# A cached attention step with a gated MLP: the per-head sums behind the next unit's first turns, and the MLP's first half at the head

## The chip, the cores and the metric

The kernel runs on one core of a Trainium2 chip. The metric is device time in microseconds for one execution; a profiled execution also gives a span, from the first to the last instruction. The engines are TensorE (PE, with its weight loads PEld), VectorE (DVE), ScalarE (ACT), GpSimd (POOL) and SyncE (SP), which here only issues transfers. They run on their own and meet through semaphores.

## The reference

```python
x  = A_x                                   # 2 rows of 512, bfloat16
xn = layernorm(x)
# attention over a cache: 2 batches, 32 query heads, 8 key heads, 32768 positions, head width 128
q = (xn @ wq)                              # 512 -> 4096
p = softmax(q . k_cache / sqrt(128))       # 4 query heads share a key head
s = (p @ v_cache) @ wo                     # 4096 -> 512
# MLP on one position: the shifted heads are all padding, so w1 and w2 add nothing
x1 = xn                                    # B: x + hs, hs = 0
h2 = gelu(layernorm(x1) @ w3) @ w4         # 512 -> 1792 -> 512, gelu by tanh
out = x + s * silu(x1 + h2)
```

With one position per sequence the shift by one or two positions leaves zeros, so `hs` is zero and the kernel reads neither w1 nor w2.

## The kernel before, in words

The caches are 16 units, one for each pair of batch and key head; unit n has batch n % 2 and key head n // 2. Each unit has 8192 KB of K and 8192 KB of V. A partition holds 256 positions; the layout in memory is position-major, so a transfer is a plain copy.

**Buffers.** `kbuf` has room for three halves of a K (each of CW = 16384 columns); even units use the first two thirds, odd units the last two, and the shared third is worked on first. `vbuf` holds one V, no more. The weights borrow these: wq lies in the last third of `kbuf` until the queries are made; w3 and w4 lie in the first third and wo in the second once the last units are through with them.

**Head.** `layernorm` (L364), transposition of xn and of its normalised copy (`xT`), the setting up of selection matrices and the clearing of PSUM tiles on VectorE (L400 to L418), then `q_job` (L420): 128 narrow matmuls in a loop, a selection by `pick`, a copy to `qp` (L447) and a clearing of hP (L449). `place_q(n)` (L451) puts the four query heads of unit n into `qz`, where zeros stand around them, by four copies on ScalarE, one for each block of 32 partitions.

**A unit** (loop at L547):

- `scores(n)` (L459): two halves of four turns. A turn (L465) is a transposition of 32x32 blocks on VectorE from `kbuf` to one of two buffers `ktb`; eight matmuls (L477) with `qz` follow on TensorE. So turn t + 2 waits for the scores of turn t.
- `load_k(n + 1)` is issued by SyncE once the four turns of the first half have read the shared third.
- `softmax(n)` (L486): `place_q(n + 1)`, maximum (L490), a transposition of the maxima, their spread over partitions, exp with sums on ScalarE (L500), the transposition pT (L506), 1/sum (rS, L507).
- `values(n)` (L509): 64 matmuls from `vbuf` into `acc`. `load_v(n + 1)` is issued when they end, as `vbuf` is then free.
- `unit_end(n)` (L527): VectorE multiplies `acc` by rS and a mask (acs, L530) and adds four parts (acr, L534); TensorE makes the heads' outputs (ot, L537) and ScalarE copies them into oQ (L539).

**Order.** Every engine works in the order in which the operations were recorded. `Plan.op` finds the waits from the regions read and written; `emit_looped` folds equal rounds of TensorE (each unit) and VectorE (each pair of units, the last pair written out) into loops, in which `fit` writes a wait's value as a line in the loop's counters. All loads of K, V and weights stand in one SyncE stream in this order: wq, K(0), V(0), K(1), V(1), ..., K(15) in two halves, V(15), w3, w4, four pieces of wo, the output.

**Tail.** After the last unit: `mlp_in` (L569, 16 matmuls with w3 into hP), the turn of oQ (oT, L581), perm (L585), gelu in six operations on ScalarE and VectorE (L590 to L597), its transposition `h_turn` (L600) and copy h_bf (L606), `mlp_out` (L610) with w4, the wo products (`wo_rows`, `wo_last`) between them, the gate, the product and the two output transfers.

Of the kernel before, what the change touches and what calls it, by code (L numbers as in the profile page):

```python
# [8 lines left out]
BF16 = mybir.dt.bfloat16  # L9
U32 = mybir.dt.uint32  # L10
ACT = mybir.ActivationFunctionType
ALU = mybir.AluOpType
# [14 lines left out]
class Plan:  # L27
# [69 lines left out]
    def fit(self, points, first):  # L97

        i1 = min(i for i, _ in points if i > first)
        line, early, ahead = {}, {}, {}  # L100
        for s in sorted({s for (i, _), w in points.items() if i > first for s in w}):
            js = sorted({j for (i, j), w in points.items() if i == i1 and s in w})
            step = self.step[s]
            if js != sorted({j for i, j in points if i == i1}):
                assert js == [0]
                early[s] = (points[i1, 0][s] - (i1 - first) * step, step)
                got = {k: early[s][0] + (k[0] - first) * step for k in points if k[1] == 0}
            else:
                v0 = points[i1, js[0]][s]
                jstep = points[i1, js[1]][s] - v0 if len(js) > 1 else 0  # L110
                line[s] = (v0 - (i1 - first) * step, step, jstep)
                got = {k: line[s][0] + (k[0] - first) * step + k[1] * jstep for k in points}
            for k, v in got.items():
                if k[0] > first:
                    assert points[k].get(s) == v, (s, k, v, points[k])
                assert v > 0
                if k[0] == first and points[k].get(s, 0) > v:
                    ahead[s] = max(ahead.get(s, 0), points[k][s])
        for k, w in points.items():
            for s, v in w.items():  # L120
                if k[0] == first and s not in line and s not in early:
                    ahead[s] = max(ahead.get(s, 0), v)
        return line, early, ahead

    def emit_looped(self, eng, kind):
# [22 lines left out]
        for seg in segments:  # L148
            fits = []
            for q, places in enumerate(seg):  # L150
                assert len({r[p].label for r in rounds for p in places}) == 1
                line, early, a = self.fit(
                    {(i, j): r[p].waits for i, r in enumerate(rounds) for j, p in enumerate(places)}, 0)
                assert not early or q == 0
                fits.append((line, early))
# [9 lines left out]
        with self.nc.Fori(0, len(rounds), 1, engines=[kind], hint_back_edge=True) as i:  # L165
            for seg, fits in zip(segments, plans):
                if len(seg[0]) == 1:
                    o, (line, _) = rounds[0][seg[0][0]], fits[0]
                    self.emit_one(o, [(s, i * step + base) for s, (base, step, _) in line.items()])
                    continue  # L170
                for s, (base, step) in fits[0][1].items():
                    e.wait_ge(self.sems[s], i * step + base)
                with self.nc.Fori(0, len(seg[0]), 1, engines=[kind]) as j:
                    for places, (line, _) in zip(seg, fits):
# [9 lines left out]
def kernel(  # L184
# [38 lines left out]
    W4 = DK * Fdim  # L223
    HW = NHALF * GT * 32 // 2
    assert NCH == 2 and NB == NS and NU % 2 == 0 and FK <= 16 and W4 + FK * D <= CW
# [8 lines left out]
    def sb(name, shape, dt, align=32):  # L234
        return nc.alloc_sbuf_tensor(name, shape, dt, align_bytes=align).ap()
# [15 lines left out]
    qz = sb("qz", [128, 4, QW], BF16)  # L251
    qp = sb("qp", [128, 4, B, Hkv, rep], BF16)
# [12 lines left out]
    oQ = sb("oQ", [128, B, NR], BF16)  # L265
    oT = sb("oT", [128, B, NR], BF16)
# [184 lines left out]
    def place_q(n):  # L451
        b, g = n % 2, min(n // 2, Hkv - 1)
        for i in range(4):
            c0 = 32 - rep + 32 * i
            act(lambda i=i, c0=c0: A.copy(  # L455
                out=qz[32 * i:32 * i + 32, :, c0:c0 + rep], in_=qp[32 * i:32 * i + 32, :, b, g, :]),
                ["qp"], [("qz", i, i + 1)])

    def scores(n):  # L459
        for h, c in enumerate(halves(n % 2)):  # L460
            P.inner = h
            for t in range(NB // KG):
                i = t % KTB
# [63 lines left out]
    def unit_end(n):  # L527
        b, g = n % 2, n // 2
        ot = mA[:, 136:136 + rep]
# [6 lines left out]
            ["acs"], ["acr"], "acr")  # L536
        pe(lambda: T.matmul(ot, lhsT=acr[:, :], rhs=headm[:, :], start=True, stop=True),  # L537
           ["acr", "headm"], ["mA"], "ot")
        act(lambda: A.copy(out=oQ[:, b, g * rep:(g + 1) * rep], in_=ot), ["mA"], [("oQ", n, n + 1)])  # L539

    q_job()
    place_q(0)

# [3 lines left out]
    for n in range(NU):  # L547
# [3 lines left out]
        if n + 1 < NU:  # L551
            load_k(n + 1)
        softmax(n)
# [3 lines left out]
        unit_end(n)  # L557
        for s in ("PE", "DVE", "ACT"):
# [9 lines left out]

    def mlp_in():  # L569
        w3 = w3_s.rearrange("p k (q f) -> p k f q", f=FK)  # L570
        for k in range(DK):
            for j in range(4):
                f0, f1 = 4 * j, min(4 * j + 4, FK)
                r = T.matmul(
                    hP[32 * j:32 * j + B, 0:(f1 - f0) * 128].rearrange("p (f q) -> p f q", q=128),
                    lhsT=xT[:, DK + k, :], rhs=w3[:, k, f0:f1, :],
                    start=(k == 0), stop=(k == DK - 1), tile_position=(0, 32 * j))
        return r

    pe(mlp_in, [kreg(0, W4), "xT"], ["hP"])  # L580
    dve(lambda: V.transpose(  # L581
        out=oT[:, :, :].rearrange("p b r -> p (b r)"), in_=oQ[:, :, :].rearrange("p b h -> p (b h)")),
        ["oQ"], ["oT"])
    oPp = mA[:, 0:B * NR]
    pe(lambda: T.matmul(  # L585
        oPp, lhsT=perm[:, :, :].rearrange("p h a -> p (h a)"),
        rhs=oT[:, :, :].rearrange("p b r -> p (b r)"), start=True, stop=True), ["perm", "oT"], ["mA"])
    dve(lambda: V.tensor_copy(out=oP[:, :, :].rearrange("p b r -> p (b r)"), in_=oPp), ["mA"], ["oP"])

    act(lambda: A.activation(out=x2[:, :], in_=hP[:, :], func=ACT.Square), ["hP"], ["x2"])  # L590
    dve(lambda: V.tensor_scalar(
        out=x2[:, :], in0=x2[:, :], scalar1=0.044715, scalar2=1.0, op0=ALU.mult, op1=ALU.add), ["x2"], ["x2"])
    dve(lambda: V.tensor_mul(out=x2[:, :], in0=hP[:, :], in1=x2[:, :]), ["hP", "x2"], ["x2"])
    act(lambda: A.activation(out=th[:, :], in_=x2[:, :], func=ACT.Tanh, scale=GELU_C), ["x2"], ["th"])
    dve(lambda: V.tensor_scalar(
        out=th[:, :], in0=th[:, :], scalar1=0.5, scalar2=0.5, op0=ALU.mult, op1=ALU.add), ["th"], ["th"])
    dve(lambda: V.tensor_mul(out=h_row[:, :], in0=hP[:, :], in1=th[:, :]), ["hP", "th"], ["h_row"])  # L597
    hT = hP.bitcast(BF16)[:, 0:512]

    def h_turn():  # L600
        for s in range(4):
            r = T.transpose(out=hT[:, s * 128:(s + 1) * 128], in_=h_row[:, s * 128:(s + 1) * 128], identity=ident[:, :])
        return r

    pe(h_turn, ["h_row", "ident"], ["hP"])
    dve(lambda: V.tensor_copy(  # L606
        out=h_bf[:, :, :].rearrange("p (j s) b -> p j s b", j=4),
        in_=hT.rearrange("p (s j c) -> p j s c", s=4, j=4)[:, :, :, 0:B]), ["hP"], ["h_bf"])
# [39 lines left out]
    pe(mlp_out, [kreg(W4, FK * D), "h_bf"], ["mD"])  # L648
# [60 lines left out]
```

## Time and profile before

| | us |
|---|---|
| median of three runs | 667.06 (665.47 to 668.28) |
| the profiled execution | 667.29 |
| its span | 665.5 |
| PE busy | 412.8 |
| DVE busy | 381.0 |
| ACT busy | 41.3 |
| POOL busy | 2.0 |
| HBM read | 280.50 MB, 421 GB/s over the span |

A row of the timeline reads: start, length, engine, line of the kernel, operation, output <- input with shapes, count of merged instructions, and in brackets the engine's idle time before it with what ended it. A row of the chain has start, length, and what was worked or waited on. For transfers the profile gives the issue (an instruction of SyncE of 0.3 to 0.6 us) and the time from issue to landing.

### The profile page before, as it was taken

To read this page: it belongs to the slowest core of one execution; us is meant where nothing else is said; L and a number is where in the kernel's file an instruction comes from. 1 tells how busy PE (TensorE), PEld (TensorE's weight loads), DVE (VectorE), ACT (ScalarE), POOL (GpSimd) and SP (SyncE) were. 2 spreads that over 40 slices of the span, in tenths; PEclk is the share of its full clock that TensorE was granted. 3 is DMA by queue.
4 is the path that set the end of the run, shared out by engine and by line. 5 is a ranking of instruction groups with operands and counts; after the bars stand their busy time and mean duration, and the time that the engine had idled before them with its cause. 6 is when DMAs were issued, how large, how long until landed. Compare 5 with 4: busy or idle time off the path is not lost.

```text
span 665.5 us, 6187 instructions
## 1 busy us (share of the span) xinstructions
PE 412.8 (62%) x2397; PEld 162.9 (24%) x2397; DVE 381.0 (57%) x304; ACT 41.3 (6%) x124; POOL 2.0 (0%) x11
## 2 busy tenths in 40 slices
PE   1766764856746485664658466464847646485864
PEld 1532221322212132221223222121312212132321
DVE  5057673827457382745748284673828467385833
ACT  1001010010101001010100101010010101001011
POOL 1000000000000000000000000000000000000000
PEclk9999897877779787786968778797977879797877
DMA  9999999999999999999999999999999999999992
GB/s 379 441 441 390 390 421 437 441 441 441 441 441 430 390 441 441 441 441 441 418 402 441 441 441 441 441 441 441 418 402 441 441 441 441 441 410 473 418 397 101
DMA packets 5815, 280.55 MB, mean 422 GB/s; under 512 B 682, under 2 KB 692, under 8 KB 948
## 3 DMA queue, kind: packets, MB, share of 16 engines
q1 hardware_dynamic: 5768, 280.50, 97.7%
q8 instruction: 2, 0.03, 0.0%
q10 hardware_dynamic: 44, 0.01, 0.0%
q14 instruction: 1, 0.01, 0.0%
HBM read 280.50 MB, written 0.00 MB: 421 GB/s over the span
## 4 chain that ended last, share of the span: by engine, by line
DMA 55%; PE 19%; DVE 18%; issue 6%; ACT 1%; another core or an unknown queue 1%; DVEq 0%; ACTq 0%; SPq 0%
DMA kbuf<-in_A_k_cache_dram 55%; DVE ktb L465 14%; PE sc L477 12%; PE mA L428 3%; PE acc L518 2%; DVE m L490 1%; ACT pr L500 1%; PE wP L631 0%; DVE pT L506 0%; DVE acs L530 0%; DVE acr L534 0%; PE mD L613 0%; DMA x_bf<-in_A_x_dram 0%; DVE stats L366 0%
## 5 line engine op out<-in xcount | busy, mean ns | idle before, releaser
L477 PE MATMUL sc<-ktb,qz 128*128 128x512 bf16 x1024 | 272.5, 416 | 124.6 <-DVE ktb L465 122.4
L465 DVE STREAM_TRANSPOSE ktb<-kbuf 128x2048 uint32<-128x2048 uint32 x128 | 286.5, 2287 | 84.9 <-DMA kbuf<-in_A_k_cache_dram 59.0
L477 PEld LDWEIGHTS sc<-ktb,qz 128*128 128x128 bf16 x1024 | 96.9, 103 | 293.8 <-issue 152.4
L518 PE MATMUL acc<-vbuf,pT 128*16 128x512 bf16 x1024 | 86.4, 512 | 13.7 <-DVE rS L507 13.7
L530 DVE SCALAR_TENSOR_TENSOR acs<-acc,rS,mask 128x512 f32<-128x512 f32 x16 | 12.0, 751 | 88.7 <-PE acc L518 88.7
L518 PEld LDWEIGHTS acc<-vbuf,pT 128*16 128x16 bf16 x1024 | 31.0, 113 | 62.5 <-issue 52.4
L455 ACT COPY qz<-qp 32x16 bf16<-32x16 bf16 x68 | 13.7, 201 | 426.9 <-PE sc L477 393.4
L490 DVE TENSOR_REDUCE m<-sc 128x1 f32<-128x1024 f32 x16 | 19.6, 1224 | 32.0 <-PE sc L477 32.0
L506 DVE STREAM_TRANSPOSE pT<-pr 128x1024 bf16<-128x1024 bf16 x16 | 19.9, 1245 | 20.4 <-ACT pr L500 20.4
L537 PE MATMUL mA<-headm,acr 128*128 128x4 f32 x32 | 6.3, 268 | 30.7 <-DVE acr L534 30.7
L428 PE MATMUL mA<-xT,kbuf 128*128 128x2 bf16 x128 | 17.7, 183 | 11.7 <-issue 6.7
L503 PE MATMUL mA<-S,headf 128*128 128x1 f32 x32 | 7.9, 318 | 23.8 <-ACT pr L500 23.8
L500 ACT ACTIVATE pr<-sc,nb 128x1024 bf16<-128x1024 f32 x16 | 17.8, 1114 | 29.5 <-DVE nb L499 29.5
L491 PE MATMUL mA<-identf,m 128*1 128x128 f32 x16 | 4.3, 270 | 21.1 <-DVE m L490 21.1
L428 PEld LDWEIGHTS mA<-xT,kbuf 128*128 x128 | 13.3, 104 | 16.1 <-issue 13.1
L534 DVE TENSOR_REDUCE acr<-acs 128x128 f32<-128x512 f32 x16 | 16.3, 1018 | 0.6
L537 PEld LDWEIGHTS mA<-headm,acr 128*128 128x128 f32 x32 | 4.9, 194 | 38.8 <-DVE acr L534 38.8
L435 DVE CAST q_sb<-mA 128x64 bf16<-128x64 f32 x1 | 0.2, 225 | 24.8 <-PE mA L428 24.8
L503 PEld LDWEIGHTS mA<-S,headf 128*128 128x128 f32 x32 | 6.6, 257 | 25.2 <-ACT pr L500 25.2
L496 PE MATMUL mA<-ones_f,gx 1*128 1x1 f32 x32 | 6.5, 268 | 9.9 <-DVE gx L494 9.9
L539 ACT CAST oQ<-mA 128x4 bf16<-128x4 f32 x16 | 2.6, 162 | 146.6 <-PE mA L537 146.6
L491 PEld LDWEIGHTS mA<-identf,m 128*1 128x1 f32 x16 | 1.3, 79 | 29.0 <-DVE m L490 29.0
(84 smaller groups left out, 63.3 us busy)
## 6 DMA issues: line engine op xcount, KB each, us to landing
kbuf<-in_A_k_cache_dram SPq DMA_DIRECT2D x2, 4096.0 KB, 22.6
kbuf<-in_A_wq_dram SPq DMA_DIRECT2D x1, 4096.0 KB, 12.2
kbuf<-in_B_w_dram SPq DMA_DIRECT2D x2, 1792.0 KB, 30.7
kbuf<-in_A_wo_dram SPq DMA_DIRECT2D x1, 2048.0 KB, 32.0
kbuf<-in_A_wo_dram SPq DMA_DIRECT2D x1, 1280.0 KB, 29.4
kbuf<-in_A_wo_dram SPq DMA_DIRECT2D x1, 512.0 KB, 30.2
vbuf<-in_A_v_cache_dram SPq DMA_DIRECT2D x16, 25.6
kbuf<-in_A_wo_dram SPq DMA_DIRECT2D x1, 256.0 KB, 30.4
```

The lines of the kernel that those rows point to most:

```text
L428: r = T.matmul(qT[:, bass.ds(h2 * (2 * B) + e * B, B)], lhsT=kb[:, bass.ds(h2 * (2 * Dh) + (2 * CW + k * HD + e * Dh), Dh)], rhs=xT[:, k, ...
L455: act(lambda i=i, c0=c0: A.copy(out=qz[32 * i:32 * i + 32, :, c0:c0 + rep], in_=qp[32 * i:32 * i + 32, :, b, g, :]), ["qp"], [("qz", i, i ...
L465: dve(lambda i=i, c0=c0: V.transpose(out=ktb[i][:, :], in_=kbuf[:, c0:c0 + KG * GT * Dh].bitcast(U32)), [kreg(c0, KG * GT * Dh)], [f"ktb{i ...
L477: r = T.matmul(sc[:, bass.ds(half, HW)].rearrange("p (t k) -> p t k", k=32), lhsT=qz[:, k, off:off + 128], rhs=kv[:, k // 2, k % 2, :, :], ...
L490: dve(lambda: V.tensor_reduce(out=m1[:, :], in_=sc[:, :], axis=AX.X, op=ALU.max), ["sc"], ["m1"], "max")
L500: act(lambda: A.activation(out=pr[:, :], in_=sc[:, :], func=ACT.Exp, bias=nb[:, 0:1], scale=inv_sqrt_dh, accum_out=S1[:, :]), ["sc", "nb"] ...
L503: pe(lambda: T.matmul(sS, lhsT=headf[:, :, :].rearrange("p x h -> p (x h)"), rhs=S1[:, :], start=True, stop=True), ["headf", "S1"], [rO], "S")
L506: dve(lambda: V.transpose(out=pT[:, :, :].rearrange("p t r -> p (t r)"), in_=pr[:, :]), ["pr"], ["pT"], "pT")
L518: r = T.matmul(acc[32 * j:32 * j + 16, :].rearrange("p (i d) -> p i d", d=Dh), lhsT=pT[:, half * GT + u, r0:r0 + 16], rhs=vv[:, x, u, :, : ...
L530: dve(lambda: V.scalar_tensor_tensor(out=acs[:, :, :], in0=acc[:, :].rearrange("p (i d) -> p i d", d=Dh), scalar=rS[:, 0:1], in1=mask[:, : ...
L534: dve(lambda: V.tensor_reduce(out=acr[:, :], in_=acs[:, :, :].rearrange("p i d -> p d i"), axis=AX.X, op=ALU.add), ["acs"], ["acr"], "acr")
L537: pe(lambda: T.matmul(ot, lhsT=acr[:, :], rhs=headm[:, :], start=True, stop=True), ["acr", "headm"], ["mA"], "ot")
```

## The change

- `unit_end` is split. `unit_sum(n)` (acs and acr) is recorded within `scores(n + 1)`, behind the second turn of its first half; `unit_out(n)` (ot and its copy) behind those scores and ahead of `softmax(n + 1)`. Unit 0 so works on an empty unit before it, whose product goes to a spare tile; rS is cleared for it. The last unit's sums come after the loop.
- w3 is loaded behind wq into the first half of `vbuf`. V(0) comes in two halves: the second half (c = 1) behind K(0), the first one behind `mlp_in`, which now follows the first `place_q`.
- gelu's six operations are recorded right after the loop, so they follow exp(15) on ScalarE and rS(15) on VectorE. `h_turn` and h_bf stand ahead of the last `unit_sum`.
- w4 goes to the start of `kbuf` and is loaded directly behind V(15).
- `place_q` is one multiplication on GpSimd, of `qp` spread over four blocks by the new mask qm, made by a reduction on VectorE at the head.
- `fit` no longer has a separate list of waits ahead of an inner loop: a wait found for the first pass alone is written with step zero.

```diff
+    def load_v0_half(c):
+        load("v", vbuf[:, c * CW:(c + 1) * CW], cache(A_v_cache, 0)[:, c * CW:(c + 1) * CW],
+             [("vbuf", c * CW, (c + 1) * CW)])
...
-    w3_s = kbuf[:, 0:W4].rearrange("p (k f) -> p k f", k=DK)
-    w4_s = kbuf[:, W4:W4 + FK * D].rearrange("p (f d) -> p f d", f=FK)
+    w3_s = vbuf[:, 0:W3].rearrange("p (k f) -> p k f", k=DK)
+    w4_s = kbuf[:, 0:FK * D].rearrange("p (f d) -> p f d", f=FK)
 
     load("wq", wq_s, wq_v, [kreg(2 * CW, CW)])
+    load("w3", w3_s, w3_v, [("vbuf", 0, W3)])
     load_k(0)
-    load_v(0)
+
+    load_v0_half(1)
...
+    dve(lambda: V.tensor_reduce(
+        out=qm[:, :], in_=identf[:, :].rearrange("p (i w) -> p i w", i=4), axis=AX.X, op=ALU.max),
+        ["identf"], ["qm"])
+    dve(lambda: V.memset(rS[:, :], 0.0), [], ["rS"])
...
     def place_q(n):
         b, g = n % 2, min(n // 2, Hkv - 1)
-        for i in range(4):
-            c0 = 32 - rep + 32 * i
-            act(lambda i=i, c0=c0: A.copy(
-                out=qz[32 * i:32 * i + 32, :, c0:c0 + rep], in_=qp[32 * i:32 * i + 32, :, b, g, :]),
-                ["qp"], [("qz", i, i + 1)])
+        pool(lambda: G.tensor_tensor(
+            out=qz[:, :, 32 - rep:].rearrange("p k (i w) -> p k i w", w=32)[:, :, :, 0:rep],
+            in0=qp[:, :, b, g, :].unsqueeze(2).to_broadcast([128, 4, 4, rep]),
+            in1=qm[:, :].unsqueeze(1).unsqueeze(3).to_broadcast([128, 4, 4, rep]), op=ALU.mult),
+            ["qp", "qm"], ["qz"])
...
             for t in range(NB // KG):
+                if h == 0 and t == KTB:
+                    unit_sum(n - 1)
...
     q_job()
     place_q(0)
+    mlp_in()
+    load_v0_half(0)
...
         scores(n)
         if n + 1 < NU:
             load_k(n + 1)
+        unit_out(n - 1)
         softmax(n)
         values(n)
         if n + 1 < NU:
             load_v(n + 1)
-        unit_end(n)
...
-    load("w3", w3_s, w3_v, [kreg(0, W4)])
-    load("w4", w4_s, w4_v, [kreg(W4, FK * D)])
+    gelu()
+    load("w4", w4_s, w4_v, [kreg(0, FK * D)])
...
-    pe(mlp_in, [kreg(0, W4), "xT"], ["hP"])
...
+    pe(h_turn, ["h_row", "ident"], ["hP"])
...
+    unit_sum(NU - 1)
+    unit_out(NU - 1)
...
-    pe(mlp_out, [kreg(W4, FK * D), "h_bf"], ["mD"])
+    pe(mlp_out, [kreg(0, FK * D), "h_bf"], ["mD"])
```

More of the change, by code (lines that the diff above doesn't have):

```diff
@@ L99, in fit @@
         i1 = min(i for i, _ in points if i > first)
-        line, early, ahead = {}, {}, {}
+        line, ahead = {}, {}
         for s in sorted({s for (i, _), w in points.items() if i > first for s in w}):
@@ L103, in fit @@
             step = self.step[s]
[L104 to L112, printed above, removed]
+            assert js in ([0], sorted({j for i, j in points if i == i1}))
+            v0 = points[i1, 0][s]
+            jstep = points[i1, js[1]][s] - v0 if len(js) > 1 else 0
+            line[s] = (v0 - (i1 - first) * step, step, jstep)
+            got = {k: line[s][0] + (k[0] - first) * step + k[1] * jstep for k in points if k[1] in js}
             for k, v in got.items():
@@ L120, in fit @@
             for s, v in w.items():
-                if k[0] == first and s not in line and s not in early:
+                if k[0] == first and s not in line:
                     ahead[s] = max(ahead.get(s, 0), v)
-        return line, early, ahead
+        return line, ahead
     def emit_looped(self, eng, kind):
@@ L151, in emit_looped @@
                 assert len({r[p].label for r in rounds for p in places}) == 1
-                line, early, a = self.fit(
+                line, a = self.fit(
                     {(i, j): r[p].waits for i, r in enumerate(rounds) for j, p in enumerate(places)}, 0)
-                assert not early or q == 0
-                fits.append((line, early))
+                fits.append(line)
                 for s, v in a.items():
@@ L265 @@
     oQ = sb("oQ", [128, B, NR], BF16)
+    oJ = sb("oJ", [128, rep], BF16)
     oT = sb("oT", [128, B, NR], BF16)
@@ L556 @@
             load_v(n + 1)
-        unit_end(n)
-        for s in ("PE", "DVE", "ACT"):
+        for s in ("PE", "DVE", "ACT", "POOL"):
             got = P.count[s] - before.get(s, 0)
@@ L567 @@
         load(f"wo{i}", kbuf[:, c0:c1], wo_v[:, r0 * D:r1 * D], [kreg(c0, c1 - c0)])
[L569 to L578, printed above, removed]
-    pe(mlp_in, [kreg(0, W4), "xT"], ["hP"])
[L581 to L608, printed above, removed]
     def mlp_out():
@@ L646, in wo_last, with h_turn @@
         pe(fn, ["oP", kreg(CW + r0 * D, (r1 - r0) * D)], ["s_ps"])
-    pe(mlp_out, [kreg(W4, FK * D), "h_bf"], ["mD"])
+    hT = hP.bitcast(BF16)[:, 0:512]
+    def h_turn():
+        for s in range(4):
+            r = T.transpose(out=hT[:, s * 128:(s + 1) * 128], in_=h_row[:, s * 128:(s + 1) * 128], identity=ident[:, :])
+        return r
+    pe(h_turn, ["h_row", "ident"], ["hP"])
+    dve(lambda: V.tensor_copy(
+        out=h_bf[:, :, :].rearrange("p (j s) b -> p j s b", j=4),
+        in_=hT.rearrange("p (s j c) -> p j s c", s=4, j=4)[:, :, :, 0:B]), ["hP"], ["h_bf"])
+    unit_sum(NU - 1)
+    unit_out(NU - 1)
+    dve(lambda: V.transpose(
+        out=oT[:, :, :].rearrange("p b r -> p (b r)"), in_=oQ[:, :, :].rearrange("p b h -> p (b h)")),
+        ["oQ"], ["oT"])
+    oPp = mA[:, 0:B * NR]
+    pe(lambda: T.matmul(
+        oPp, lhsT=perm[:, :, :].rearrange("p h a -> p (h a)"),
+        rhs=oT[:, :, :].rearrange("p b r -> p (b r)"), start=True, stop=True), ["perm", "oT"], ["mA"])
+    dve(lambda: V.tensor_copy(out=oP[:, :, :].rearrange("p b r -> p (b r)"), in_=oPp), ["mA"], ["oP"])
+    pe(mlp_out, [kreg(0, FK * D), "h_bf"], ["mD"])
     dve(lambda: V.tensor_copy(out=th[:, :], in_=mD[:, :]), ["mD"], ["th"])
```

42 lines of the change are left out of this document (32 added, 10 removed).

## The prediction

> **What bounds the kernel now.** I read the page first (span, chain by line, sizes of transfers), then the issues and landings of single transfers, then the chain and the timeline.
>
> ```profile
> span 665.5 us, 6187 instructions
> ...
> DMA kbuf<-in_A_k_cache_dram 55%; DVE ktb L465 14%; PE sc L477 12%; PE mA L428 3%; PE acc L518 2%; DVE m L490 1%; ACT pr L500 1%; PE wP L631 0%; DVE pT L506 0%; DVE acs L530 0%; DVE acr L534 0%; PE mD L613 0%; DMA x_bf<-in_A_x_dram 0%; DVE stats L366 0%
> ...
> kbuf<-in_B_w_dram SPq DMA_DIRECT2D x2, 1792.0 KB, 30.7
> ```
>
> Over half the chain is the landing of K. The chain's own rows (start, length) and one row of SyncE's timeline show how regular that is:
>
> ```profile
> 124.02 27.60 DMA kbuf<-in_A_k_cache_dram
> ...
> 162.32 27.91 DMA kbuf<-in_A_k_cache_dram
> ```
>
> ```profile
> 146.02 0.33 SPq L313 DMA_DIRECT2D vbuf<-in_A_v_cache_dram  x1
> ```
>
> K(3) lands at 151.62, K(4) at 190.23: 38.61 us for one K and one V, so **19.3 us for each 8192 KB** in a queue that never runs dry. V(3) is issued at 146.02, 5.6 us before K(3) lands, so the next transfer always stands ready. At the head it does not. Here the first row of each pair has the issue time, the second the time to landing (in the first pair the largest of the three is V(0)'s):
>
> ```profile
> L313 SPq DMA_DIRECT2D vbuf<-in_A_v_cache_dram x1: 577/577/577, 1.9 to 1.9; - x1
> DMA to landing us min/median/max: 31.0/40.5/49.9
> ...
> L313 SPq DMA_DIRECT2D kbuf<-in_A_k_cache_dram x1: 328/328/328, 50.5 to 50.5; - x1
> DMA to landing us min/median/max: 21.7/21.7/21.7
> ...
> L313 SPq DMA_DIRECT2D vbuf<-in_A_v_cache_dram x1: 328/328/328, 71.7 to 71.7; - x1
> DMA to landing us min/median/max: 21.9/21.9/21.9
> ```
>
> V(0) lands at 51.8, K(1) at 72.2, V(1) at 93.6. K(1) took 20.4 us behind V(0) and V(1) 21.4 behind K(1): **3.2 us of empty queue** beyond 2 × 19.3. An idle queue needs 21.7 − 19.3 = 2.4 to 21.9 − 19.3 = 2.6 us from issue to flow, so a transfer must be issued 2.5 us before its forerunner lands.
>
> The tail, from the same two kinds of rows and the timeline:
>
> ```profile
> L313 SPq DMA_DIRECT2D vbuf<-in_A_v_cache_dram x1: 328/328/328, 610.2 to 610.2; - x1
> DMA to landing us min/median/max: 24.9/24.9/24.9
> ...
> L313 SPq DMA_DIRECT2D kbuf<-in_A_wo_dram x2: 432/432/433, 622.6 to 623.1; - x2
> DMA to landing us min/median/max: 30.2/30.3/30.4
> ```
>
> ```profile
> 611.11 1.02 DVE L534 TENSOR_REDUCE acr<-acs 128x128 f32<-128x512 f32 x1
> ...
> 612.04 4.49 DVE L465 STREAM_TRANSPOSE ktb<-kbuf 128x2048 uint32<-128x2048 uint32 x2
> ...
> 619.91 11.16 DVE L465 STREAM_TRANSPOSE ktb<-kbuf 128x2048 uint32<-128x2048 uint32 x5 [0.40 <-PE sc L477]
> ...
> 633.07 1.23 DVE L490 TENSOR_REDUCE m<-sc 128x1 f32<-128x1024 f32 x1 [2.00 <-PE sc L477]
> ...
> 638.46 5.80 PE L518 MATMUL acc<-vbuf,pT 128*16 128x512 bf16 x64 [0.77 <-DVE rS L507]
> ...
> 644.39 0.75 DVE L530 SCALAR_TENSOR_TENSOR acs<-acc,rS,mask 128x512 f32<-128x512 f32 x1 [6.00 <-PE acc L518]
> ...
> 646.72 3.87 PE L574 MATMUL hP<-kbuf,xT 128*2 128x512 bf16 x16
> ...
> 647.02 0.24 DVE L581 STREAM_TRANSPOSE oT<-oQ 128x64 bf16<-128x64 bf16 x1 [0.84 <-ACT oQ L539]
> ...
> 650.52 0.20 PE L585 MATMUL mA<-oT,perm 128*128 128x64 bf16 x1
> ...
> 654.32 0.61 PE L602 MATMUL hP<-ident,h_row 128*128 128x128 bf16 x4 [3.60 <-DVE h_row L597]
> ...
> 654.97 0.17 DVE L606 COPY h_bf<-hP 128x32 bf16<-128x32 bf16 x1 [0.70 <-PE hP L602]
> ...
> 655.20 1.87 PE L613 MATMUL mD<-kbuf,h_bf 128*2 128x512 bf16 x14 [0.27 <-DVE h_bf L606]
> ...
> 661.30 0.30 PE L642 MATMUL s_ps<-kbuf,oP 128*2 128x128 bf16 x8
> ...
> 662.29 0.65 SPq L313 DMA_DIRECT2D out_dram<-out_bf  x1
> ```
>
> V(15) lands at 635.1, the last piece of wo at 653.5 (623.1 + 30.4). Yet the last values start only at 638.46, released by rS, 3.3 us after V(15); and the output leaves 8.8 us after wo. So the tail is not bound by transfers but by compute: late scores, then mlp_in, gelu and mlp_out in a row.
>
> **The change, part by part.**
>
> *Head.* The transfers become wq, w3, K(0), half of V(0), and, once mlp_in has read w3, the other half. w3 costs 1792/8192 × 19.3 = 4.2 us of queue, so the first half lands at 51.8 + 4.2 − 9.65 = 46.4. When can the second be issued?
>
> ```profile
> 9.68 0.37 DVE L404 TENSOR_REDUCE headm<-identf 128x4 f32<-128x128 f32 x1
> ...
> 13.34 0.17 DVE L418 MEMSET mA<- 128x128 f32 x1
> ...
> 13.88 1.12 PE L428 MATMUL mA<-xT,kbuf 128*128 128x2 bf16 x8 [5.03 <-DVE mA L418]
> ...
> 39.59 0.48 DVE L449 MEMSET hP<- 128x512 f32 x1 [0.18 <-DVE qp L447]
> 39.98 4.47 DVE L465 STREAM_TRANSPOSE ktb<-kbuf 128x2048 uint32<-128x2048 uint32 x2
> ...
> 45.93 13.36 DVE L465 STREAM_TRANSPOSE ktb<-kbuf 128x2048 uint32<-128x2048 uint32 x6 [1.48 <-PE sc L477]
> ```
>
> The q job waits for VectorE's last memset, not for wq, so the new reduction for qm (0.37, as headm) and the one-column memset (at most 0.17) shift it by 0.5 us. mlp_in follows the memset of hP: 39.59 + 0.48 + 0.5 = 40.6. Its 16 matmuls took 3.87 us in the tail, where I find the same tile shapes; that the array may be quicker here bounds it below by the 1.87 of the 14 matmuls of L613. I take 3.87, the same instruction. The issue is then at 44.5, flow at 47.0, 0.6 us after the first half has landed (none with the short value). V(0) is whole at 56.7, K(1) lands at 76.0 if issued by 54.2. Turns: two end at 40.5 + 4.5 = 45.0; acs and acr of the empty unit follow (0.75 + 1.02 with a gap, to 46.9); scores of turn 0 run behind mlp_in and take at most 3.7 us (42.2 to 45.9 now) and at least what they take later, when they keep up with turns of 2.23: 46.7 to 48.2. I take the early end, since mlp_in has the array busy just before; the late one would put another 0.5 us on V(1). Turn 2 starts at 46.9, 1 us late, so K(1) is issued at 51.5, in time. Everything of unit 0 behind that is 1 us late: V(1) is issued at 72.7, flows at 75.2, before K(1) lands. V(1) lands at 76.0 + 19.3 = 95.3, **1.7 us later** than before (1.1 with the short mlp_in): w3's 4.2 us minus 3.2 of holes filled, plus 0.6.
>
> *Units 1 to 14.* The sums come after the second turn:
>
> ```profile
> 583.34 2.31 DVE L465 STREAM_TRANSPOSE ktb<-kbuf 128x2048 uint32<-128x2048 uint32 x1 [1.64 <-PE sc L477]
> ```
>
> Turn 2 waited 1.64 us for scores there anyway; acs and acr take 1.8, so the turn and the K issue come 0.2 us later. The matmul ot now stands ahead of the transposition of the maxima, its oQ copy with it; both lie beside the 1.2 us maximum. Price nothing against the 5.6 − 2.5 = 3.1 us to spare at each V issue. Nor is anything gained: the queue sets 38.6 us per unit. GpSimd's placing replaces four ACT copies. No row shows this operation:
>
> ```profile
> 2.41 0.62 POOL L357 MEMSET qz<- 128x624 bf16 x1
> ```
>
> By that row 64 elements cost at most 0.6 us; if ten times slower per element still about 0.6. The cover is 4.5 us of mlp_in for unit 0 and the whole softmax and values later. I take zero.
>
> *Unit 15.* V(15) lands 1.7 later, at 636.8. The old order kept VectorE from turning K(15) until values(14) and their sums were done (612.04). Now two turns are done during values(14). Values(14), 1.9 us later than before, end at 612.1; scores follow at once, sums to 614.0, then six turns of 2.23 us to 627.4 (K(15)'s second half, 19.3 ahead of V(15), is there at 617.5, before the fifth turn at 618.5) and the last scores by 629.4, against 633.07 now. From there to rS takes 638.46 − 633.07 = 5.4: ready at 634.8. So **V(15) becomes the last wait**: values start at 637.0, a gain of 1.5.
>
> *Tail.* gelu needs Square, two VectorE operations, Tanh, two more: from the end of mlp_in (650.6) to h_row (654.3) 3.7 us. Its start is free at exp(15), near 633, VectorE's part behind rS at 634.8; it ends by 638.6, and the cover is values to 642.8. If the cover shrank, at most 3.7 would return. Gone from the path are mlp_in and gelu; behind the values stand now, in PE's order, h_turn (0.65 to h_bf) and h_bf (0.17), of which about 0.7 lie ahead of acs. From the start of the values S: acs S + 5.93 + 0.7; oT ends 2.87 later (644.39 to 647.26), perm 0.25 more, mlp_out at S + 9.75. From mlp_out to the output issue 655.20 to 662.29 = 7.09. Before: S + 23.83; now S + 16.84: **7.0 gained**. w4 and wo follow V(15) without w3: the last piece lands at 653.5 + 1.7 − 4.2 = 651.0, needed 6.1 after mlp_out at 652.9. It is in time, with 1.9 to spare.
>
> *Sum.* The profiled execution took 667.29 (span 665.5 plus 1.8), the median of the three runs is 667.06. Gain 1.5 + 7.0 = 8.5: 658.8 for such an execution, 658.6 to 658.8 beside the median. I say 658.7.
>
> **Rivals.**
>
> *A: the array stays warm in the tail, and wo's landing becomes the bound.*
>
> ```profile
> 646.00:648.00 2.00, 1.76 (x11) 0.80 (x15) 0.43 (x2) 0.16 (x1) 0.00 (x0) 0.58 1.01 431
> ```
>
> The granted clock (third figure from the end) was 0.58 right after the two idle microseconds or so behind values(15), whose last matmul ends at 644.3, so mlp_out will start cold, as before. If instead h_turn, ot and perm keep the clock up, mlp_out and the wo products shrink by up to half of 5.1 us; then the output leaves 0.99 (661.30 to 662.29) after wo at 651.0: 1.8 us earlier, 656.9. [...]
>
> *B: scores(15) don't start earlier* (PE busy or turns held elsewhere). Then rS stays the last wait, at 638.46 + 1.7: S = 640.2 and the time 662. For it: one stall of over 2.2 us would do it (637.0 − 634.8). Against: K(15) lands long before, and nothing else is queued on VectorE.
>
> *C: the head costs more* than 1.7: every microsecond that mlp_in or the placing ends later moves all landings by one. With 3 more: 662.
>
> *D, slower than before: GpSimd and VectorE shut each other out.* place_q stands exactly where VectorE starts the maximum and the softmax copies. If the multiplication took p us and held VectorE, each unit's way from K to the next V issue would grow by p. Below p = 3.1 us the queue hides it; beyond, 14 units each pay p − 3.1. The gain is gone at p = 3.7, and at p = 4 the time is 671. For it: broadcast operands on an engine of which the trace shows only memsets and one select. Against: the memset row, 0.62 us for ten times the elements. [...]
>
> **How the numbers follow.** Forecast 0.66 (its own range 657.5 to 660.5), A 0.12, B or C 0.12, no effect beyond 0.5% (B and C together, and part of the tail's gain lost) 0.04, D 0.06. A measurement of this kernel can tell about 0.5% from no change. Range: from A with the short mlp_in and no hole (656.9 − 0.6 − some 0.5) to B or C (662 and a little): 655.8 to 662.5. Chances: faster 0.90, same 0.04, slower 0.06.
>
> **What would show it.** V(1) should land at 95.3 with at most 0.6 us of hole before the second half of V(0); landings every 19.3 us after; turn 2 released by acr, not by scores; values(15) released by V(15)'s landing near 637.0; no gelu between values and mlp_out; mlp_out near 646.8; output issue near 653.8. Wrong if V(1) lands after 97, if rS releases the last values, if mlp_out waits for w4, or if GpSimd's operation takes over 3 us.

## The result, and the profile after

The changed kernel takes 658.9 us (median; 658.57 to 660.1) against 667.17 for the kernel before on the same chip (665.47 to 668.69): a ratio of 0.9877, with a 95% interval of 0.986 to 0.9894. The forecast was 658.7. The execution that the rows below come from took 658.78.

The page of the changed kernel, first its span, then the chain by line, then the group of the new multiplication on GpSimd:

```profile
span 657.0 us, 6163 instructions
...
DMA kbuf<-in_A_k_cache_dram 61%; DVE ktb L472 13%; PE sc L484 10%; DMA kbuf<-in_A_wo_dram 5%; PE mA L433 3%; DVE acs L535 0%; PE wP L626 0%; DVE stats L367 0%; DMA x_bf<-in_A_x_dram 0%; DVE acr L539 0%; DVE xf L363 0%; DVE wsum L675 0%; PE s_ps L616 0%; DVE ln L373 0%; DVE xn L373 0%
...
L458 POOL TENSOR_TENSOR qz<-qp,qm 128x64 bf16<-128x64 bf16 x17 | 5.0, 293 | 621.9 <-PE sc L484 585.3
```

Before, the chain ended in values(15) and the MLP, and no landing of wo stood in it. Now wo's landing stands in it with 5%, and neither values (acc) nor softmax (m, pr, pT) is in it any more. The multiplication costs 0.293 us.

Issues and times to landing of the changed kernel, in the order: first half of V(0) (the one behind `mlp_in`), K(1), V(1), V(15), then the first and the second piece of wo:

```profile
L308 SPq DMA_DIRECT2D vbuf<-in_A_v_cache_dram x1: 328/328/328, 44.2 to 44.2; - x1
DMA to landing us min/median/max: 12.1/12.1/12.1
...
L308 SPq DMA_DIRECT2D kbuf<-in_A_k_cache_dram x1: 328/328/328, 50.8 to 50.8; - x1
DMA to landing us min/median/max: 24.7/24.7/24.7
...
L308 SPq DMA_DIRECT2D vbuf<-in_A_v_cache_dram x1: 328/328/328, 72.1 to 72.1; - x1
DMA to landing us min/median/max: 23.3/23.3/23.3
...
L308 SPq DMA_DIRECT2D vbuf<-in_A_v_cache_dram x1: 328/328/328, 611.3 to 611.3; - x1
DMA to landing us min/median/max: 25.8/25.8/25.8
...
L308 SPq DMA_DIRECT2D kbuf<-in_A_wo_dram x1: 328/328/328, 612.6 to 612.6; - x1
DMA to landing us min/median/max: 34.6/34.6/34.6
...
L308 SPq DMA_DIRECT2D kbuf<-in_A_wo_dram x1: 328/328/328, 618.7 to 618.7; - x1
DMA to landing us min/median/max: 31.5/31.5/31.5
```

V(0) is whole at 56.3, K(1) lands at 75.5, V(1) at 95.4, V(15) at 637.1; from V(1) to V(15) it is 541.7, against 541.5 before (635.1 − 93.6). So w3 and the empty unit's sums cost 1.8 us at the head together, and the units between neither gain nor lose. wo's first piece lands at 647.2, its second at 650.2.

The timeline of the changed kernel, from `mlp_in` at the head to the output:

```profile
40.33 3.81 PE L557 MATMUL hP<-vbuf,xT 128*2 128x512 bf16 x16 [1.18 <-DVE hP L454]
...
585.30 4.50 DVE L472 STREAM_TRANSPOSE ktb<-kbuf 128x2048 uint32<-128x2048 uint32 x2
...
608.04 4.50 DVE L472 STREAM_TRANSPOSE ktb<-kbuf 128x2048 uint32<-128x2048 uint32 x2 [1.97 <-DMA kbuf<-in_A_k_cache_dram]
...
629.60 1.23 DVE L497 TENSOR_REDUCE m<-sc 128x1 f32<-128x1024 f32 x1 [2.00 <-PE sc L484]
...
634.78 0.13 DVE L514 RECIPROCAL rS<-mA 128x1 f32<-128x1 f32 x1
...
637.08 4.96 PE L525 MATMUL acc<-vbuf,pT 128*16 128x512 bf16 x64 [2.86 <-DVE th L571]
637.11 0.69 DVE L573 TENSOR_TENSOR h_row<-hP,th 128x512 bf16<-128x512 f32 x1
...
641.97 0.40 PE L647 MATMUL hP<-ident,h_row 128*128 128x128 bf16 x4
...
645.40 1.03 PE L608 MATMUL mD<-kbuf,h_bf 128*2 128x512 bf16 x14
...
647.27 1.88 PE L626 MATMUL wP<-kbuf,oP 128*2 128x512 bf16 x16 [0.84 <-DVE th L667]
...
650.24 1.45 PE L626 MATMUL wP<-kbuf,oP 128*2 128x512 bf16 x10 [0.66 <-DMA kbuf<-in_A_wo_dram]
...
653.97 0.64 SPq L308 DMA_DIRECT2D out_dram<-out_bf  x1
```

Three readings need care. The last values are said to be released by th (L571), which doesn't feed them; they start with V(15)'s landing. The products of wo's first piece (647.27) are said to be released by th (L667), which they don't read either; they start with that piece's landing at 647.2. And the wait for wo at 650.24 is only 0.66 long, because TensorE has just done other work: what counts is that the rest of the tail hangs on this landing. mlp_out comes 3.4 us behind the values and takes 1.03 us instead of 1.87; the granted clock (third figure from the end; 0.50 from 655.2 to 656.4 in the kernel before) shows why. Windows of the changed kernel in the tail, each with busy times, clock, share of the DMA engines and GB/s:

```profile
644.00:646.00 2.00, 1.12 (x15) 0.68 (x17) 0.76 (x3) 1.21 (x2) 0.00 (x0) 1.00 0.99 409
646.00:648.00 2.00, 1.16 (x15) 0.28 (x12) 0.69 (x1) 0.23 (x1) 0.00 (x0) 0.66 0.96 410
```

The array was still at full clock after two idle microseconds (1.00 from 642.4 to 644.35) and dropped only behind mlp_out, at 646.65; it stayed at half clock (0.50) from there to the output.

### The profile page after: what moved, and what is told of

Same layout as the page of the kernel before. It is cut to its first block, busy times and chain, and to the rows that moved or that the text cites. A ratio compares the mean times of both kernels' runs of the same rounds, so it can differ in the third digit from the quotient of the medians.

```text
span 657.0 us, 6163 instructions
## 1 busy us (share of the span) xinstructions
PE 406.4 (62%) x2399; PEld 163.0 (25%) x2399; DVE 382.0 (58%) x308; ACT 27.7 (4%) x57; POOL 7.0 (1%) x28
## 4 chain that ended last, share of the span: by engine, by line
DMA 66%; DVE 15%; PE 13%; issue 5%; DVEq 0%; ACT 0%; ACTq 0%; SPq 0%
DMA kbuf<-in_A_k_cache_dram 61%; DVE ktb L472 13%; PE sc L484 10%; DMA kbuf<-in_A_wo_dram 5%; PE mA L433 3%; DVE acs L535 0%; PE wP L626 0%; DVE stats L367 0%; DMA x_bf<-in_A_x_dram 0%; DVE acr L539 0%; DVE xf L363 0%; DVE wsum L675 0%; PE s_ps L616 0%; DVE ln L373 0%; DVE xn L373 0%
## 5 line engine op out<-in xcount | busy, mean ns | idle before, releaser
L458 POOL TENSOR_TENSOR qz<-qp,qm 128x64 bf16<-128x64 bf16 x17 | 5.0, 293 | 621.9 <-PE sc L484 585.3
L503 PEld LDWEIGHTS mA<-ones_f,gx 1*128 1x128 f32 x32 | 4.9, 192 | 13.0 <-DVE gx L501 13.0
L499 DVE TENSOR_REDUCE gm<-mA 1x4 f32<-1x128 f32 x16 | 4.5, 278 | 5.8 <-PE mA L498 5.8
L546 PEld LDWEIGHTS mA<-headm,acr 128*128 128x128 f32 x34 | 6.3, 187 | 4.6 <-DVE acr L539 2.1
```

The costliest lines, as they stand in the source:

```text
L503: pe(lambda: T.matmul(bc, lhsT=gx[:, :, :].rearrange("o x h -> o (x h)"), rhs=ones_f[0:1, 0:1], start=True, stop=True), ["gx", "ones_f"], ...
```

## The experiments

After this trace my theory **"wo"** was: the end is set by the landing of wo's second piece and 3.8 us of work behind it (650.2 to 653.97). Its rival **"compute"**: the end is still the row of work from the values to the output, as the prediction had it, and the waits for wo only take up slack. The expectations name the two so. All ratios are to the kernel before on the same chip.

**Without w4's load** (mlp_out then works on what is left in `kbuf`; the MLP's second half is left out of the result):

```diff
-    load("w4", w4_s, w4_v, [kreg(0, FK * D)])
```

> The changed kernel without the load of w4 (left out: mlp_out multiplies by what lies in that stretch of kbuf). Theory 'wo': the tail now waits for wo's landings (second piece 650.2, output 3.8 later), so wo comes 4.2 us earlier, the wait before the second piece's products goes and the output leaves 1.5 to 3 us earlier: 656 to 657.4. Rival 'compute' (the tail as forecast, bound by the chain from the last values): nothing changes, 658.6 to 659.2.

Measured: 657.61 (655.8 to 660.35), 0.985 (0.9803 to 0.9897). The four times fall into two pairs, near 656 and near 660. The profiled execution belongs to the second pair (659.19); its tail, and one window of it:

```profile
647.05 1.86 PE L607 MATMUL mD<-kbuf,h_bf 128*2 128x512 bf16 x13
...
654.33 0.64 SPq L308 DMA_DIRECT2D out_dram<-out_bf  x1
```

```profile
646.00:648.00 2.00, 1.47 (x15) 0.75 (x19) 0.47 (x2) 1.45 (x2) 0.00 (x0) 0.50 0.10 34
```

No wait for wo is left, and DMA is nearly idle (0.10). But the clock is at half (0.50), and from mlp_out to the output it takes 7.28: "compute" holds in this execution. The other pair, of which there is no trace, has the time that "wo" expected. The two theories are thus not exclusive; that the clock, which differs between executions, decides which one binds is likely and not shown by this run.

**gelu, its transposition and h_bf behind the last oP copy**, as late as before:

```diff
-    gelu()
     load("w4", w4_s, w4_v, [kreg(0, FK * D)])
...
+    gelu()
+    pe(h_turn, ["h_row", "ident"], ["hP"])
```

> The changed kernel with gelu, h_turn and h_bf behind the copy oP, as before. mlp_out comes 4.4 us later (3.7 of gelu, 0.65 of h_turn and h_bf, minus what h_turn held up ahead of acs). Theory 'wo': 1.5 us of that fall into the two waits for wo (0.84 and 0.66), so +2.9: 661.8. Rival 'compute': the whole 4.4, 663.3. If gelu's cover were worth nothing: 658.9.

Measured: 662.24 (660.82 to 662.76), 0.9925 (0.9898 to 0.9951). So gelu's place is worth some 3.3 us of the whole (662.24 − 658.9). In its timeline gelu delays mlp_out by 3.7 us, and the output by 2.0:

```profile
649.06 1.87 PE L607 MATMUL mD<-kbuf,h_bf 128*2 128x512 bf16 x14 [0.27 <-DVE h_bf L662]
...
655.96 0.64 SPq L308 DMA_DIRECT2D out_dram<-out_bf  x1
```

3.7 of work taken away gave 2.0 to 3.3. The traces show the rest as wo's wait: with gelu late mlp_out to output takes 6.90 with no wait for wo, though its mlp_out took 1.87 instead of 1.03, against 8.57 with wo's waits. The median stands between the two theories (nearer to "wo").

**The sums back at the end of their unit** (the last unit written out of TensorE's loop):

```diff
-                if h == 0 and t == KTB:
-                    unit_sum(n - 1)
...
-        unit_out(n - 1)
...
             load_v(n + 1)
+            unit_sum(n)
+            unit_out(n)
```

> The changed kernel with the sums and the head product of units 0 to 14 at the unit's end, as before (unit 15 written out behind TensorE's loop). The last values start at rS again, 638.5 + 1.9 = 640.3, which is 3.2 later. Theory 'wo': 1.5 of it hidden, +1.7: 660.6. Rival 'compute': 662.1. If the sums' place did not matter: 658.9. Landings of K and V as in the changed kernel.

Measured: 659.91 (657.85 to 660.76), 0.9881 (0.9843 to 0.9919), by its times not to be told from the changed kernel. Its timeline shows where the 3.7 us go by which its values start later:

```profile
640.82 5.89 PE L523 MATMUL acc<-vbuf,pT 128*16 128x512 bf16 x64 [0.69 <-DVE rS L512]
...
650.07 1.03 PE L607 MATMUL mD<-kbuf,h_bf 128*2 128x512 bf16 x14
...
655.17 0.64 SPq L308 DMA_DIRECT2D out_dram<-out_bf  x1
```

rS releases the values again, 3.7 us later than V(15) does in the changed kernel; mlp_out is 4.7 later, the output only 1.2: from mlp_out to the output it takes 5.10 at full clock (mlp_out 1.03, the products of wo's first piece 1.24 instead of 1.88), without a wait for wo. The sums' early place does what was forecast for unit 15, and in this pair of traces 3.5 us of it are lost again between mlp_out and the output. That is wo's wait and the half clock together (8.57 against 5.10); the pair doesn't separate them.

**The four ScalarE copies instead of GpSimd's multiplication:**

```diff
-        pool(lambda: G.tensor_tensor(
+        for i in range(4):
+            act(lambda i=i, c0=c0: A.copy(
```

> The changed kernel with the queries placed by four ScalarE copies, as before. Both theories: 658.9, within 0.5, since 0.88 us of copies lie beside a maximum and a softmax chain of 2.8 us. If GpSimd's 0.29 us per unit cost or saved anything through VectorE, it would show as a multiple of 15 times that, 4 us or so.

Measured: 658.41 (657.76 to 659.88), 0.9872 (0.9838 to 0.9907). An effect of 4 us is ruled out. The move to GpSimd shows neither a cost nor a gain, within an interval of some 2 us to either side.

**One part alone on the kernel before.** First the move of the sums, with `unit_sum` and `unit_out` as in the change:

```diff
+                if h == 0 and t == KTB:
+                    unit_sum(n - 1)
...
-        unit_end(n)
```

> The kernel before with the sums and the head product alone moved behind the next unit's second turn. The last values start when V(15) has landed, 635.2 instead of 638.46, and the tail of before follows whole: 3.2 us faster, 663.9. If this part did nothing without the others: 667.2.

Measured: 664.49 (663.82 to 665.97), 0.995 (0.9931 to 0.9968). The values now wait for V:

```profile
636.70 6.44 PE L515 MATMUL acc<-vbuf,pT 128*16 128x512 bf16 x64 [2.88 <-DMA vbuf<-in_A_v_cache_dram]
```

Of the 3.3 us by which V(15) once was too early, 1.8 are gained; V(15) itself is 1.6 later than before (636.7 against 635.1) with no w3 ahead of it. The empty unit's sums at the head alone do that, by delaying the turns of unit 0: V(1) is issued at 73.7 instead of 71.7 and lands at 95.6 instead of 93.6 (one trace each).

Then w3 and `mlp_in` at the head alone, with V(0) in halves:

```diff
+    load("w3", w3_s, w3_v, [("vbuf", 0, W4)])
     load_k(0)
-    load_v(0)
+    load_v0_half(1)
...
+    mlp_in()
+    load_v0_half(0)
```

> The kernel before with w3 and mlp_in alone moved to the head, and V(0) in halves. V(15) lands 1.8 later (4.2 of w3 less the holes filled), the values start at rS, 640.3, and the tail loses mlp_in: mlp_out 13.3 behind the values' start instead of 16.7. In all 1.6 faster: 665.6. Rival: w3's 4.2 us all come back at the end and nothing is gained, 667.2 or more.

Measured: 665.34 (663.72 to 666.87), 0.9959 (0.9945 to 0.9974). Here rS still releases the values, 0.4 later than before:

```profile
638.89 5.56 PE L516 MATMUL acc<-vbuf,pT 128*16 128x512 bf16 x64 [0.77 <-DVE rS L505]
```

The expected time is met, two of its marks are not: the values were to start at 640.3, and V(15) is 1.3 later than before, not 1.8. V(1) lands at 94.8, so w3 and `mlp_in` without the empty unit's sums cost 1.2 us at the head.

The two parts give 0.5% and 0.4%, the whole 1.2%. The experiment with gelu late prices the third part at 0.5%; gelu's early place needs `mlp_in` at the head.

**wo in other pieces** (rows up to 16, 24, 28, 32 instead of 16, 26, 30, 32), so that the second piece lands earlier:

```diff
-    wo_cuts = [0, NR // 2, NR - 6, NR - 2, NR]
+    wo_cuts = [0, NR // 2, NR - 8, NR - 4, NR]
```

> The changed kernel with wo cut at rows 16, 24, 28 instead of 16, 26, 30. Theory 'wo': the second piece lands 0.6 us earlier, its products are fewer, and the last piece's landing (652.0) decides: 0.5 us faster than the changed kernel, 658.4. Rival 'compute': no change or slower by the 0.3 us of more narrow products, 659.2.

Measured: 658.59 (657.99 to 660.07), 0.9865 (0.9848 to 0.9882).

```profile
651.97 0.60 PE L637 MATMUL s_ps<-kbuf,oP 128*2 128x128 bf16 x16 [0.60 <-DMA kbuf<-in_A_wo_dram]
...
653.27 0.64 SPq L308 DMA_DIRECT2D out_dram<-out_bf  x1
```

The wait moved to the last piece, with 1.3 us behind it. **The changed kernel again**, beside it:

> The changed kernel once more beside the others of this call: 658.9 by both theories. Its trace tells whether the warm array and the late first piece of wo of the first profile come back: theory 'wo' expects the second piece of wo as the last landing waited for in either case.

Measured: 659.84 (657.91 to 660.11), 0.9879 (0.9862 to 0.9895). The wait for the second piece is there again, with 3.0 us from its products' start to the output (3.7 in the first trace):

```profile
650.10 1.02 PE L626 MATMUL wP<-kbuf,oP 128*2 128x512 bf16 x10 [0.66 <-DMA kbuf<-in_A_wo_dram]
...
653.11 0.64 SPq L308 DMA_DIRECT2D out_dram<-out_bf  x1
```

The other cuts are not to be told from these.

**The array kept busy in the gaps** (eight matmuls into a part of `sc` that nothing reads any more):

```diff
+    def keep(n):
+        def fn():
+            for _ in range(n):
+                r = T.matmul(sc[:, 0:512], lhsT=ident[:, :], rhs=ktb[0][:, 0:256].bitcast(BF16), start=True, stop=True)
...
     pe(h_turn, ["h_row", "ident"], ["hP"])
+    keep(6)
...
     unit_out(NU - 1)
+    keep(2)
```

> The changed kernel with six idle matmuls behind h_turn and two behind the last ot, into a part of sc that nothing reads any more, so that the array has work between the last values and mlp_out. Theory 'clock and wo': in most executions the clock is still full at mlp_out anyway, and where it is not, these matmuls keep it; wo's landing is then the bound in every execution: 658.5, and no run near 660. Rival 'compute alone': the clock makes no difference or the idle matmuls delay ot: 659 to 660.

Measured: 658.21 (657.93 to 659.75), 0.9866 (0.9849 to 0.9884). The median is that of "clock and wo", but one run of the four is near 660. And the trace shows another reason than wo for the unchanged time:

```profile
637.89 6.55 PE L525 MATMUL acc<-vbuf,pT 128*16 128x512 bf16 x64 [2.85 <-DVE th L571]
...
647.80 1.03 PE L608 MATMUL mD<-kbuf,h_bf 128*2 128x512 bf16 x14
...
652.93 0.64 SPq L308 DMA_DIRECT2D out_dram<-out_bf  x1
```

The values, which lie ahead of the idle matmuls, ran at half clock until 643.85 and took 6.55 instead of 4.96, so mlp_out came 2.4 us later than in the changed kernel. From there to the output it took 5.13 at full clock (1.00 from 644 to 648, the products of wo's first piece 1.24) instead of 8.57. The second piece of wo, landed at 650.0, was not waited for; only the third was, for 0.48.

The same with **w4's load left out as well** (again the MLP's second half is missing):

```diff
+    keep(6)
...
-    load("w4", w4_s, w4_v, [kreg(0, FK * D)])
```

> The same without the load of w4 (mlp_out multiplies by what lies in kbuf), so that wo is there before it is needed. Without the idle matmuls this gave 655.8, 656.0, 659.2 and 660.4. Theory 'clock and wo': all runs near 656. If those four runs differed for another reason than the clock, the spread stays and the median is near 657.6.

Measured: 656.7 (655.05 to 657.1), 0.9829 (0.9813 to 0.9845). The two pairs of the first experiment have become one group, from 4.6 us the spread has shrunk to 2.1, and the median lies between the two expectations. That the busy array did this is not shown: the kernel before spread by 4.7 us on the first experiment's chip (665.15 to 669.81) and by 2.2 on this one (666.67 to 668.82). A window of the kernel with w4, then the tail of the one without:

```profile
646.00:648.00 2.00, 1.23 (x10) 0.54 (x13) 1.03 (x3) 0.81 (x2) 0.00 (x0) 1.00 0.99 413
```

```profile
647.08 1.03 PE L607 MATMUL mD<-kbuf,h_bf 128*2 128x512 bf16 x14
...
652.17 0.64 SPq L308 DMA_DIRECT2D out_dram<-out_bf  x1
```

At full clock (1.00 from 644 to 648, the products of wo's first piece 1.24) and with wo there, mlp_out to output takes 5.09. So between these two traces the clock is worth 2.2 us of it (7.28 − 5.09). Taking w4's bytes away, with the busy array in both, gives 1.5 (658.21 − 656.7), half of the 3.0 between the changed kernel and the first experiment's lower pair. **Both, the busy array and the other cuts:**

```diff
+    keep(6)
...
-    wo_cuts = [0, NR // 2, NR - 6, NR - 2, NR]
+    wo_cuts = [0, NR // 2, NR - 8, NR - 4, NR]
```

> The idle matmuls with wo cut at rows 16, 24, 28. Theory: bound by the last landing of wo and 1.3 us behind it: 658.0, 0.5 below the first of this call. If the cut is worth nothing: the same as the first of this call.

Measured: 658.55 (657.63 to 659.3), 0.9863 (0.9845 to 0.988). No better than either. None of these is clearly below the changed kernel. In this last trace wo binds (its last piece lands at 652.65, the output leaves at 653.79); with the busy array alone wo and compute ended together.

**Without w3's load** (the MLP's first half is left out; GpSimd clears the place, so `mlp_in` multiplies zeros). Two theories of the head: "order" says that V(1) comes when unit 0's work lets it be issued, whatever w3's bytes; "bytes" says that w3's 4.2 us come off.

```diff
-    load("w3", w3_s, w3_v, [("vbuf", 0, W3)])
...
+    pool(lambda: G.memset(vbuf[:, 0:W3], 0.0), wr=[("vbuf", 0, W3)])
```

> The changed kernel without the load of w3 (left out: mlp_in multiplies zeros, which GpSimd writes to that part of vbuf early). Theory 'order': the second part of V(0) waits for mlp_in, not for the queue, so w3's 4.2 us only fill a hole that unit 0's compute leaves anyway; V(1) and V(15) land as in the changed kernel, 658.9. Rival 'bytes': the queue is the bound from the start, and everything lands up to 4.2 us earlier: 655.

Measured: 665.09 (664.7 to 665.58), 0.9963 (0.995 to 0.9976): 6 us slower than "order" expected, 10 slower than "bytes". The cause is in the first microseconds of this kernel:

```profile
2.64 6.68 DVE L363 CAST xf<-x_bf 2x512 f32<-2x512 bf16 x1 [2.64 <-DMA x_bf<-in_A_x_dram]
2.97 6.07 POOL L358 MEMSET vbuf<- 128x7168 bf16 x1
```

and, for comparison, the same cast in the kernel before:

```profile
2.66 0.64 DVE L362 CAST xf<-x_bf 2x512 f32<-2x512 bf16 x1 [2.66 <-DMA x_bf<-in_A_x_dram]
```

VectorE's small cast ended 0.28 us behind GpSimd's clearing, 6.0 us late, and the whole head came late with it. The 0.64 us of before show the same on a small scale: there GpSimd's clearing of `qz` (2.41 to 3.03) runs beside it, and the cast ends 0.27 us behind that. In the changed kernel the cast starts at 2.25, takes 1.06 and again ends 0.28 behind it. The row of this kernel's V(1):

```profile
L308 SPq DMA_DIRECT2D vbuf<-in_A_v_cache_dram x1: 327/327/327, 79.0 to 79.0; - x1
DMA to landing us min/median/max: 22.5/22.5/22.5
```

V(1) lands at 101.5, 6.1 later than in the changed kernel, though the queue had 4.2 us less to move. But the experiment can't decide between the theories: it delayed unit 0's work by 6 us, and with that delay the order of issue binds whatever w3's bytes cost. What the bytes alone cost stays open.

## Why the prediction was right, and where it was not

- **Head: right in sum.** V(1) was forecast at 95.3 and landed at 95.4 in this trace (95.4 to 96.8 in the eight traces with the same head). Two small errors cancelled: everything ran 0.3 to 0.7 earlier than forecast (`mlp_in` at 40.33, not 40.6; the first half of V(0) issued at 44.2, not 44.5; K(1) landing at 75.5, not 76.0), and V(1) then flowed with a hole of 0.6 (95.4 − 75.5 − 19.3) although it had been issued 3.4 us ahead. That 2.5 us ahead suffice is thus not exact. That the empty unit's sums delay the head was right: alone they cost V(15) 1.6 (V(1) 2.0).
- **Units 1 to 14: right.** 541.7 us from V(1) to V(15). The turns behind the sums start with acr's end (585.30) and wait for no scores.
- **GpSimd's placing: right.** 0.293 us, and no effect that the ScalarE variant shows. That VectorE's work can stand behind GpSimd's, as rival D had it, showed at one place of these kernels: the cast at the head ended 0.27 to 0.28 us behind the memset that GpSimd had running, whether it so took 0.64 (before), 1.06 (the changed kernel) or 6.68 us (without w3). The multiplication shows nothing of the kind: it takes 0.293 beside a maximum read from PSUM, which takes 1.224 us on average in both kernels. What sets the two apart no run isolated.
- **Unit 15: right.** Turns during values(14), last scores at 629.6 (forecast 629.4), rS at 634.78 (634.8), values with V(15) at 637.08 (637.0). gelu ends at 637.8 and is hidden whole.
- **Tail: right in sum, wrong in two terms.** From the start S of the values to the output issue 16.84 was forecast and 16.89 measured. But mlp_out came at S + 8.32, not S + 9.75, and from there to the output it took 8.57, not 7.09. The first error is the clock (0.50 from 639.43 to 642.84 before, 1.00 from 639.82 to 646.65 in the changed kernel), carried over from before: the terms "S + 5.93 + 0.7" and "so mlp_out will start cold, as before". The values took 4.96 instead of 5.80 and the transposition 0.40 instead of 0.61, so acs came at S + 5.42; and mlp_out took 1.03 instead of 1.87. The second is the step "needed 6.1 after mlp_out at 652.9. It is in time, with 1.9 to spare": it tested only the last piece of wo. The second piece, 1280 KB, has ten products, wsum, the gather and the gate behind it, and the kernel waited for it. It landed 3.8 ahead of the output. The first piece was also late: 2048 KB should follow w4 in 4.8 us, and took 5.9, which moves the pieces behind it by 1.0 (the last one to 652.0, forecast 651.0). Without any wait for wo the way from mlp_out to the output took 7.28 even with mlp_out at half clock, so wo cost 1.3 us or more here.
- **Rival A** thus had its condition half met: the clock was up for mlp_out and down for the products of wo. Its price was wrong for the same reason as the forecast: it put the output 0.99 behind the last piece, 656.9, where the second piece gives 3.8 behind 650.2. What a clock that stays full to the end is worth with wo in place no run shows: in the kernel with the busy array the values were slower by 1.6 (6.55 against 4.96). The forecast's time stood because the row of work at half clock and wo end within a microsecond or so of each other: mlp_out at S + 9.75 and 7.09 behind it, or the second piece and 3.0 to 3.8 behind it. That the two errors cancelled was luck; the forecast was right for half of its reasons in the tail.
- **Rivals B and C** did not come about.

The tail in one line, as the traces of these kernels show it: the output leaves at the latest of mlp_out + 5.1 (clock full: 5.09 to 5.13 in three traces) or + 7.3 (clock half: 7.28 without w4), wo's second piece + 2.8 (without w3, its products 0.81) to 3.8 (the changed kernel, its products 1.45), and the last piece, in the other cuts, + 1.1 to 1.3.

## What to carry to other kernels

When work is moved off a path that ran beside transfers, test every piece of the next transfer against its first reader and the work behind that reader, not only the last piece against its own use. Take the parts one by one and together: here sums and head alone gave 0.5% and 0.4%, and gelu's place, which cannot be had alone, the rest of the 1.2% (0.5% when taken away); each gain ends where the next limit stands. A forecast that comes true can hide two errors; the marks on the way (here mlp_out's start and the piece waited for) tell, the sum doesn't.

## What the runs showed of the hardware

- **The clock behind a gap of two microseconds falls either way.** After the same gap behind the values (1.97 to 1.98 us) mlp_out took 1.03 us in five traces without idle matmuls (the changed kernel's two, the sums back, the other cuts of wo, without w3) and 1.86 in the one without w4 (13 of its 14 matmuls). With the eight idle matmuls it took 1.03 both with w4's load and without it, which five of six without them doesn't set apart. In the changed kernel the clock is at 0.50 from 632.99 to 639.82, at 1.00 from there to 646.65 and at 0.50 to the output, and mlp_out (645.40 to 646.43) just fits in; without w4 it is full from 642.38 to 645.80 (0.95 over 644 to 646, 0.50 over 646 to 648), and mlp_out comes at 647.05.

  In the tail of the kernel before the clock is full from 642.84 to 646.26, at half to 649.67, full to 653.08 and at half to 659.91. So the stretches at one clock in these two tails lasted 3.41 to 3.42 or 6.83 us. The last 3.41 us ahead of the fall at 646.65 held 1.55 us of matmuls, the stretch ahead of the fall at 646.26 in the kernel before 1.44. What decides when the clock falls or rises no run isolated. The start of the values alone doesn't tell: from 637.42 they took 5.04 us in the changed kernel's second trace, from 637.41 they took 6.30 with the busy array and without w4.
- **A fetch of instructions shows on the same DMA engines (0.9% of the 16 in one stretch).** In the changed kernel one transfer of a queue of its own falls into the stretch of wo's first piece (DMA view of the changed kernel, 641 to 647.2 us: packets, MB, share of 16 engines):

```profile
q8 instruction: 1, 0.02, 0.9%
```

  In the same stretch of the kernel before and of those with late gelu and with the head alone there is none, and there the first piece took 4.8 to 4.9 us instead of 5.9. In all profiles in which the piece took over 5 us such a fetch falls into it; but in two (the other cuts of wo, and the busy array) it does too, and the piece took 4.8. In the two kernels without w4 the fetch comes at 645.0 to 645.1 and falls into wo's third piece; there the first piece took 4.86 and the third 2.1 to 2.4 instead of 1.2. So the fetch may go with the delay and need not; no run isolated it, and the late first piece has no shown cause.
- **A hole before V(1) has no cause that I could show.** It was issued 3.4 us ahead in the changed kernel and yet 0.6 us were lost. With the other cuts of wo, whose head is the same, it was 2.0 us. K(1) has the same row there as in the changed kernel; this is V(1):

```profile
L308 SPq DMA_DIRECT2D vbuf<-in_A_v_cache_dram x1: 328/328/328, 73.0 to 73.0; - x1
DMA to landing us min/median/max: 23.8/23.8/23.8
```

  K(1) lands at 75.5 and V(1) at 96.8, 21.3 later instead of 19.3, though issued 2.5 ahead. The lead doesn't order the holes: without w4 V(1) was issued only 2.0 ahead and lost 0.8, with the head alone 3.9 ahead and lost nothing. With the clock this may make much of the spread between executions; that is not settled.
